# Top-k attention with two MoE layers on one core: order of the key rounding, the first unit's maxima, the norm's low part and the key splits

## The chip, the cores and the metric

The kernel runs on one core of one Trainium2 chip. The metric is device time in microseconds for one launch. The kernel before takes 1317.92 us, the median of three runs (1317.92 to 1319.5).

## The reference

For 4 batches of 8 heads with 576 positions of 64 elements: scores are `0.125 * q @ k.T`; in each row of scores only values not below the 32nd largest are kept; the row goes through a softmax and is multiplied with `v`. The heads are put side by side to `x` of 2304 tokens x 512. Then

```python
h = x @ w_in                      # 512 -> 2048
P = a0 + a1*h + a2*h**2 + a3*h**3
Q = 1 + |b0|*|h| + |b1|*h**2
x = (P / (Q + 1e-6)) @ w_out      # 2048 -> 512
h = x @ w_in2
out = (h * cos(h)) @ w_out2
```

All of it is float32. The second layer has weights of its own.

## The kernel before

Matrix products at full precision are made of three passes over values split into a rounded high part and a low part (`hi`, `lo`): high times high, high times low and low times high. Weights are split at the start by a converter (`conv`), which writes the low parts to DRAM, and keys by `split_k`: ScalarE rounds the raw keys into `hi`, GpSimd subtracts to get the low part, and four transfers on the queue of SyncE store both to the DRAM buffer `kdr`. The first 8 units use raw keys; later ones load the split keys back from `kdr`.

Work runs in 72 **units**. A unit is one tile of 128 queries with one pair of heads, in blocks of 8 units (four pairs by two tiles, 256 tokens). For each unit `qk` makes the scores in PSUM and ScalarE copies them to `sS`; `topk` on VectorE halves each row with a max and a min (`e<-sS`), finds the 32 largest with MAX8 and MATCH_REPLACE8, and multiplies the exponentials with the mask; `av` transposes the result on TensorE (the tiles `pp<i>a`, `pp<i>b`), copies it out (`pt`) and multiplies with `v`; `norm` divides by the sums and makes the high and low part of `x` (`xh`, `xl`). In between, each unit runs one step (256 tokens by 256 hidden columns) of each of the two layers: `in1` (products `h<-xh`, `h<-xl`), its polynomial on ScalarE, GpSimd and VectorE (`copy1`, `bias1`, `pol1`, `rec1`, `mid1`, `end1`, `low1`), `out1`, and `in2`, the cosine (`phase2`, `mid2`, `sin2`, `mul2`, `high2`, `low2`), `out2`.

Units 0 to 19 are ordered by a planner that puts ready instructions in order by a simulated time. From unit 20 to unit 71 every engine but SyncE keeps exactly the order in which `unit` writes its instructions: a wait of one holds back everything behind it on its engine. In that stretch GpSimd also waits for the last VectorE instruction written before it that shares its port, and the first VectorE instruction of a unit waits for GpSimd's last one of the unit before (`V.ahead = G.last`). That last one is `pol1`'s product `q<-q,r`.

Places that the change touches: in `unit`, the order `av`, `mid1` and `end1` (four VectorE operations and the rounding `gg<-u` on ScalarE), then `high2` (`gg<-rr`), `phase2`, the rounding of split keys, and only then the low parts kept in `low`, which are those of `norm`; `low` is filled in units 24, 32, ... and worked off in units 25, 33, 41, 49, 57 and 65, before `in1` of a new block needs `xl`. The rounding `xh<-xs` is written at the end of the unit before. `preps` says at the end of which unit raw keys are loaded for splitting; a load of an even unit is split in the odd unit behind it. For batch 2 these units are 24, 26, 28, 30 and for batch 3 40, 42, 44, 46 (so the splits are in 25, 27, 29, 31 and 41, 43, 45, 47). Units 29, 37, 45, ... also multiply the norm on GpSimd (`xs<-xs,bs`) and store a finished block from `ob`, of which there is one buffer.

The four places, in the lines of before: the rounding, `A.activation(hi, raw, AF.Copy)` in `split_k`; the table load, after the constants; `V.tensor_tensor(e[:, :, :HALF], l, r, op=ALU.max)` in `topk`; and in `unit`

```python
ev(i - UA - 1, mid1, end1)
...
for x in low:
    next(x, None)
low.clear()
```

Of the kernel before, what the change touches and what calls it, by code (L numbers as in the profile page):

```python
# [14 lines left out]
AF = mybir.ActivationFunctionType  # L15
ALU = mybir.AluOpType
# [12 lines left out]
HALF = S // 2  # L29
# [11 lines left out]
PL = 10  # L41
# [25 lines left out]
ORDER = mybir.DependencyInfo(mybir.DependencyClass.NoSync, mybir.DependencyReason.DATA)  # L67
# [52 lines left out]
def body(tc, out, qt, kt, vt, ident_d, w1_d, w1o_d, a_d, b_d, w2_d, w2o_d):  # L120
    nc = tc.nc
    V, A = InOrder(tc, nc.vector, WIN, C0), InOrder(tc, nc.scalar, WA, PA)
# [3 lines left out]
    with ExitStack() as ctx:  # L126
# [30 lines left out]
        sx = ps_s.tile([P, 2, 512], F32, name="sx")  # L157
# [5 lines left out]

        def split_k(x, b, pr):
            raw, hi = x[:, 0].bitcast(F32), x[:, 1]
            A.activation(hi, raw, AF.Copy)
            yield
            G.tensor_sub(raw, raw, hi.bitcast(F32))
            hi = hi.bitcast(F32)
            top, bot = slice(0, D), slice(D, P)  # L170
            d = kdr[b, pr]
            for o, i_ in ((d[top, 0], hi[top]), (d[bot, 0], raw[top]), (d[bot, 1], hi[bot]), (d[top, 1], raw[bot])):
                SP.dma_start(out=o, in_=i_)

        def store_k(*a):
            for _ in split_k(*a):
                pass
# [3 lines left out]
            SP.dma_start(out=x[:, 0].bitcast(F32), in_=kt[b, pr])  # L181
            return x

        qs_, vlast = {}, [None]

        def load_q(i):
            if i < nu:
                k, pr = units[i][0] // 2, units[i][1]
                raw = att.tile([P, 2, P], F32, tag="qr", bufs=QRB, name=f"qr{i}")
                A.dma_start(out=raw, in_=qt[k, pr, :, :, i % 2 * P:(i % 2 + 1) * P])  # L190
                qs_[i] = [raw, None]
# [9 lines left out]
        def low_q(i, E):  # L201
            if QH <= i < nu:
                raw, x = qs_[i]
                E.tensor_sub(x[:, 1], raw, x[:, 0].bitcast(F32))

        def load_k(i):
            n, pr = units[i]
            if i % 2 and not mixed[i]:
                ins[i] = [list(x) for x in ins[i - 1]]
                return  # L210
            ins[i] = []
            for b, _ in qts[n]:
                if n < 2:
                    k = load_k0(pr)
                else:
                    k = kv.tile([P, 2, S], F32R, tag="k", bufs=KB, name=f"k{i}_{b}")
                    A.dma_start(out=k.bitcast(F32), in_=kdr[b, pr])
                ins[i].append([k, None])
# [11 lines left out]
        load_q(0)  # L230
        load_k(0)
        load_q(1)
        ident = cst.tile([P, P], F32)
        SP.dma_start(out=ident, in_=ident_d)
        nident = cst.tile([P, P], F32R)
# [11 lines left out]
        G.memset(magic, MAGIC)  # L247
        qc = cst.tile([P, 1], F32)
        G.memset(qc, QC)
        tc.keep_in_program_order(A.preload_act_table_set("natural_log_exp_and_others"))  # L250
        na0, na1, na2, na3 = (nega[:, i:i + 1] for i in range(4))
        b0, b1 = babs[:, 0:1], babs[:, 1:2]

# [65 lines left out]
        order = [[], []]  # L319

        def halves(ap):
            return ap.rearrange("p (a c) -> p a c", a=2)

        def after(mm, bank):
            for x in order[bank]:
                tc.add_manual_dep(mm.ins, x, mybir.DependencyInfo(mybir.DependencyClass.NoSync, mybir.DependencyReason.DATA), reason="bank")

        def qk(i):
            n, pr = units[i]
            raw, x = qs_.pop(i)  # L330
            hi, lo = (x[:, 0], x[:, 1]) if x is not None else (None, None)
            kvs = ins[i]
            m = P // len(kvs)
            st[i] = sb = att.tile([P, 2, S], F32, tag="sS", bufs=SB, name=f"sS{i}")
            for j in range(2):
                rows = slice(j * D, (j + 1) * D)
                for c, (k, _) in reversed(list(enumerate(kvs))):
                    qs = slice(0, (c + 1) * m)
                    for hf in range(2):
                        o = sx[qs, hf, :HALF]  # L340
                        hs = slice(hf * HALF, (hf + 1) * HALF)
                        if n < 2:
                            mm = PE.matmul(o, raw[rows, j, qs], k[rows, 0, hs].bitcast(F32), start=True, stop=True)
                            after(mm, hf)
                        elif i < QH:
                            mm = PE.matmul(o, raw[:, j, qs], k[:, j, hs].bitcast(F32), start=True, stop=True)
                            after(mm, hf)
                        else:
                            mm = PE.matmul(o, hi[:, j, qs], k[:, j, hs], start=True, stop=False, skip_group_check=True)
                            after(mm, hf)  # L350
                            mm = PE.matmul(o, lo[:, j, qs], k[:, j, hs], start=False, stop=True, skip_group_check=True)
                        order[hf] = [mm.ins.name]
                A.activation(halves(sb[:, j]), sx[:, :, :HALF], AF.Copy)
                if j == 0:
                    yield
            if n == 1:
                store_k(kvs[0][0], 0, pr)

        def topk(i):
            n, pr = units[i]  # L360
            sc = st.pop(i)
            tiles = [sc[:, j] for j in range(2)]
            e = att.tile([P, 2, S], F32, tag="e", bufs=EB, name=f"e{i}")
            et[i] = e
            kb, t = n // 2, n % 2
            if i % 8 == 0:
                sums[kb] = sml.tile([P, 2, H], F32, tag="sum", bufs=2, name=f"sum{kb}")
            sm = sums[kb][:, t]
            hds = sml.tile([P, 2, 32], F32, tag="hd", bufs=2, name=f"hd_{i}")
            hd = [hds[:, j] for j in range(2)]  # L370
            nb = sml.tile([P, 2], F32, tag="nb", bufs=2, name=f"nb_{i}")
            big = [e[:, j, :HALF] for j in range(2)]
            both = [e[:, j] for j in range(2)]

            def top(j, x, r):
                V.max(out=hd[j][:, 8 * r:8 * r + 8], in_=x[j])

            def drop(j, x, r):
                V.match_replace(out=x[j], in_to_replace=hd[j][:, 8 * r:8 * r + 8], in_values=x[j], imm_value=NEG)

            l, r = sc[:, :, :HALF], sc[:, :, HALF:]
            grouped = U0 <= i < U1
            V.tensor_tensor(e[:, :, :HALF], l, r, op=ALU.max)
            if not grouped:
                top(0, big, 0)
                yield
            V.tensor_tensor(e[:, :, HALF:], l, r, op=ALU.min)
            if not grouped:
                top(1, big, 0)
            yield  # L390
            first = ((top, big, 0), (drop, big, 0), (top, big, 1))
            for step in (first[0 if grouped else 1:], ((drop, big, 1), (top, both, 2)), ((drop, both, 2),)):
                for f, *x in step:
                    for j in range(2):
                        f(j, *x)
                yield
            for j, s in enumerate(tiles):
                top(j, both, 3)
                if j == 0:
                    A.activation(nb, hds[:, :, 0], AF.Copy, scale=-SCALE)  # L400
                A.activation(e[:, j], s, AF.Exp, bias=nb[:, j:j + 1], scale=SCALE)
            yield
            for j, s in enumerate(tiles):
                row = sm[:, 2 * pr + j:2 * pr + j + 1]
                V.scalar_tensor_tensor(e[:, j], s, hd[j][:, 31:32], e[:, j], op0=ALU.is_ge, op1=ALU.mult, accum_out=row)
                yield
# [274 lines left out]
        def out2b():  # L681
            for part, steps in rest2:
                part(steps)
            rest2.clear()
# [68 lines left out]
        def ev(x, *fs):  # L753
            if 0 <= x < NB * NG:
                for f in fs:
                    run_event((f, *divmod(x, NG)))
# [4 lines left out]
        preps = {}  # L761
        for b in range(1, B):
            for pr in range(NP):
                preps.setdefault(16 * b - PL + pr if b == 1 else 16 * b - PL + 2 + 2 * pr, []).append((b, pr))

        nrm, low, held, split, x2, ob = [], [], [], [], [], []

# [103 lines left out]
        def unit(i, prev):  # L871
# [7 lines left out]
            a = av(i - 1)  # L879
            next(a)  # L880
            out2b()
            ev(i - UA - 1, mid1, end1)
            if not sine:
                ev(i - UB - 3, high2)
# [2 lines left out]
                    split.append(split_k(x, *a_))  # L887
                    next(split[-1])
                held.clear()
            for x in low:  # L890
                next(x, None)
            low.clear()
            low_q(i + 2, V)
            if i % 4 == 0:
                nrm.append(norm((i - 1) // 8, (i - 1) // 4 % 2))
# [70 lines left out]
        for u in range(UB + NB * NG + 3):  # L966
            grouped = U0 <= u < U1
            f = free(u, prev) if not grouped and u <= nu else iter(())
            for p in range(5):
                x = 5 * u + p  # L970
# [53 lines left out]
```

## Time and profile before

| what | value |
|---|---|
| median of three runs | 1317.92 us |
| the profiled execution's own time | 1315.85 us |
| its span in the trace | 1314.0 us |
| TensorE busy | 1225.8 us (93%) |
| VectorE busy | 1155.0 us (88%) |
| ScalarE busy | 1072.1 us (82%) |
| GpSimd busy | 586.0 us (45%) |
| mean granted TensorE clock | 0.969 |

The page divides the span into 40 slices and groups the instructions by what they read and write. Almost all lie on one line of the source (a helper that records every operation), so tiles tell them apart. The transposes `pp<i>a` mark on TensorE where the exponentials of unit i are taken up.

### The profile page before, as it was taken

To read this page: it belongs to the slowest core of one execution; us is meant where nothing else is said; L and a number is where in the kernel's file an instruction comes from. 1 tells how busy PE (TensorE), PEld (TensorE's weight loads), DVE (VectorE), ACT (ScalarE), POOL (GpSimd) and SP (SyncE) were. 2 spreads that over 40 slices of the span, in tenths; PEclk is the share of its full clock that TensorE was granted. 3 is DMA by queue.
4 is the path that set the end of the run, shared out by engine and by line. 5 is a ranking of instruction groups with operands and counts; after the bars stand their busy time and mean duration, and the time that the engine had idled before them with its cause. 6 is when DMAs were issued, how large, how long until landed. Compare 5 with 4: busy or idle time off the path is not lost.

```text
span 1314.0 us, 25152 instructions
## 1 busy us (share of the span) xinstructions
PE 1225.8 (93%) x8992; PEld 1079.5 (82%) x8992; DVE 1155.0 (88%) x2498; ACT 1072.1 (82%) x1839; POOL 586.0 (45%) x501
## 2 busy tenths in 40 slices
PE   6687788899999999999999999999999999999998
PEld 3344466678899989899989899999999999999996
DVE  6899999999899999999999899999999898756643
ACT  7887777777889888888888888988888888877753
POOL 2667556643454454545444454544454444430000
PEclk9766999999999999999999999999999999999999
DMA  8898778764367777666677776676666778867674
GB/s 292 294 345 254 246 257 276 251 240 157 130 210 231 254 253 235 205 212 230 224 240 238 240 228 200 223 230 216 218 246 251 280 275 296 289 227 249 228 269 151
DMA packets 120109, 314.99 MB, mean 240 GB/s; under 512 B 12592, under 2 KB 39344, under 8 KB 119984
## 3 DMA queue, kind: packets, MB, share of 16 engines
q1 hardware_dynamic: 86992, 261.99, 58.6%
q10 hardware_dynamic: 32992, 51.39, 12.1%
q8 instruction: 71, 1.16, 0.4%
q14 instruction: 54, 0.44, 0.1%
HBM read 278.20 MB, written 35.13 MB: 238 GB/s over the span
## 4 chain that ended last, share of the span: by engine, by line
PE 61%; DVE 12%; ACT 12%; DMA 7%; issue 4%; POOL 3%; ACTq 1%; SPq 0%; POOLq 0%; DVEq 0%
PE h L80 25%; PE o L80 11%; PE y L80 10%; PE sx L80 10%; DVE e L80 6%; DVE hd L80 3%; DMA raw<-w 2%; ACT r L80 2%; DVE u L80 2%; ACT raw L80 1%; ACT sS L80 1%; ACT e L80 1%; DMA raw<-w2o 1%; DMA kdr<-kraw 1%; PE diff L80 1%
## 5 line engine op out<-in xcount | busy, mean ns | idle before, releaser
L80 DVE MAX8 hd<-e 128x8 f32<-128x288 f32 (+1 forms) x576 | 320.5, 595 | 0.0
L80 POOL TENSOR_TENSOR gg<-rr,gg 128x512 fp32r<-128x512 f32 x56 | 72.5, 1295 | 387.1 <-DVE rr L80 184.4
L80 DVE MATCH_REPLACE8 e<-hd,e 128x288 f32<-128x288 f32 (+1 forms) x432 | 230.6, 540 | 0.0
L80 PE MATMUL o<-w2o,gg 128*128 128x512 f32 x864 | 223.6, 398 | 1.0 <-ACT ob L80 1.0
L80 PE MATMUL y<-gg,w1o 128*128 128x256 f32 x1152 | 215.2, 285 | 2.9 <-ACT gg L80 1.4
L80 PEld LDWEIGHTS y<-gg,w1o 128*128 128x128 f32 x1152 | 181.2, 191 | 6.6 <-POOL gg L80 2.6
L80 PEld LDWEIGHTS o<-w2o,gg 128*128 128x128 f32 x864 | 153.7, 189 | 28.0 <-ACT ob L80 1.2
L80 PE MATMUL h<-xh,w1hi 128*128 128x256 f32 x576 | 170.8, 297 | 3.9 <-ACT pt20a L80 0.6
L80 PE MATMUL h<-xl,w1hi 128*128 128x256 f32 x576 | 163.5, 284 | 3.5 <-DVE xl L80 3.5
L80 PE MATMUL y<-gg,w1ol 128*128 128x256 f32 x576 | 163.7, 284 | 0.0
L80 PE MATMUL h<-xh,lo 128*128 128x256 f32 x576 | 163.3, 283 | 0.0
L80 PE MATMUL h<-x2l,w2hi 128*128 128x256 f32 x576 | 161.5, 280 | 0.0
L80 PE MATMUL h<-x2h,w2hi 128*128 128x256 f32 x576 | 161.5, 281 | 0.0
L80 PE MATMUL h<-x2h,lo 128*128 128x256 f32 x576 | 161.2, 280 | 0.0
L80 DVE TENSOR_TENSOR e<-sS 128x576 f32<-128x576 f32 x144 | 115.9, 845 | 41.5 <-POOL q L80 32.9
L80 DVE SCALAR_TENSOR_TENSOR e<-sS,hd,e 128x576 f32<-128x576 f32 x144 | 126.4, 905 | 5.8 <-ACT e L80 5.8
L80 PEld LDWEIGHTS h<-xh,w1hi 128*128 128x128 f32 x576 | 109.6, 190 | 17.5 <-issue 7.1
L80 PEld LDWEIGHTS h<-xl,w1hi 128*128 128x128 f32 x576 | 109.8, 191 | 7.7 <-DVE xl L80 5.3
L80 PEld LDWEIGHTS y<-gg,w1ol 128*128 128x128 f32 x576 | 110.4, 192 | 0.4 <-issue 0.3
L80 PEld LDWEIGHTS h<-xh,lo 128*128 128x128 f32 x576 | 109.7, 190 | 0.3 <-issue 0.3
L80 PEld LDWEIGHTS h<-x2l,w2hi 128*128 128x128 f32 x576 | 108.4, 188 | 0.6 <-issue 0.2
L80 PEld LDWEIGHTS h<-x2h,w2hi 128*128 128x128 f32 x576 | 108.4, 188 | 0.4
(1025 smaller groups left out, 3240.5 us busy)
## 6 DMA issues: line engine op xcount, KB each, us to landing
w2o<-w2o SPq DMA_DIRECT2D x144, 512.0 KB, 4.3
lo<-w1lo SPq DMA_DIRECT2D x72, 512.0 KB, 3.8
w1ol<-w1ol SPq DMA_DIRECT2D x72, 512.0 KB, 4.5
lo<-w2lo SPq DMA_DIRECT2D x72, 512.0 KB, 4.4
k<-kdr ACTq DMA_DIRECT2D x44, 576.0 KB, 5.4
raw<-w SPq DMA_DIRECT2D x32, 512.0 KB, 6.1
v<-vt ACTq DMA_DIRECT2D x48, 320.0 KB, 3.8
qr<-qt ACTq DMA_DIRECT2D x72, 128.0 KB, 3.3
```

The lines of the kernel that those rows point to most:

```text
L80: r = f(*a, **k)
```

## The change

The rounding of the keys of batch 0 is ordered behind the last copy of scores made so far. ScalarE's table load is written ahead of the constants. In unit 0 the max and the min are written for each head by itself. The low part of the norm is written ahead of `mid1` and `end1`. The third and fourth pair of batches 2 and 3 are loaded for splitting in units 30 and 32, and 46 and 48, in place of 28 and 30, and 44 and 46; their splits are so in 31 and 33, and 47 and 49.

```diff
         def split_k(x, b, pr):
             raw, hi = x[:, 0].bitcast(F32), x[:, 1]
-            A.activation(hi, raw, AF.Copy)
+            r = A.activation(hi, raw, AF.Copy)
+            if b == 0:
+                tc.add_manual_dep(r.ins, copied[0], ORDER, reason="order")
             yield
...
         load_q(1)
+        tc.keep_in_program_order(A.preload_act_table_set("natural_log_exp_and_others"))
         ident = cst.tile([P, P], F32)
...
-        tc.keep_in_program_order(A.preload_act_table_set("natural_log_exp_and_others"))
         na0, na1, na2, na3 = (nega[:, i:i + 1] for i in range(4))
...
-                A.activation(halves(sb[:, j]), sx[:, :, :HALF], AF.Copy)
+                copied[0] = A.activation(halves(sb[:, j]), sx[:, :, :HALF], AF.Copy).ins.name
...
-            V.tensor_tensor(e[:, :, :HALF], l, r, op=ALU.max)
+            each = [slice(j, j + 1) for j in range(2)] if i == 0 else [slice(0, 2)]
+            for j in each:
+                V.tensor_tensor(e[:, j, :HALF], l[:, j], r[:, j], op=ALU.max)
...
-            V.tensor_tensor(e[:, :, HALF:], l, r, op=ALU.min)
+            for j in each:
+                V.tensor_tensor(e[:, j, HALF:], l[:, j], r[:, j], op=ALU.min)
...
-                preps.setdefault(16 * b - PL + pr if b == 1 else 16 * b - PL + 2 + 2 * pr, []).append((b, pr))
+                preps.setdefault(16 * b - PL + pr if b == 1 else 16 * b - PL + (2, 4, 8, 10)[pr], []).append((b, pr))
...
             out2b()
+            for x in low:
+                next(x, None)
+            low.clear()
             ev(i - UA - 1, mid1, end1)
...
-            for x in low:
-                next(x, None)
-            low.clear()
             low_q(i + 2, V)
```

## Rows read from the trace of the kernel before

**Rows 1.** Units 0-19, 20-71: length, busy PE, PEld, DVE, ACT, POOL, clock, DMA, GB/s.

```profile
0.00:330.75 330.75, 262.31 (x1369) 181.49 (x1370) 306.53 (x646) 257.42 (x485) 180.28 (x157) 0.88 0.78 260
330.75:1124.31 793.56, 780.34 (x6302) 727.70 (x6301) 743.89 (x1681) 690.21 (x1171) 381.50 (x326) 1.00 0.69 232
```

**Rows 2.** Timeline of the start: start, length, engine, operation, [idle before <- releaser].

```profile
7.12 1.28 ACT L80 ACT_TABLE_LOAD   x1
9.40 0.68 ACT L80 ACTIVATE kraw<-kraw 128x576 fp32r<-128x576 f32 x1 [1.00 <-DMA kraw<-kt]
9.99 0.63 ACT L80 ACTIVATE sS<-sx 128x576 f32<-128x576 f32 x1
...
19.30 0.63 ACT L80 ACTIVATE sS<-sx 128x576 f32<-128x576 f32 x1
...
10.65 1.43 DVE L80 TENSOR_TENSOR e<-sS 128x576 f32<-128x576 f32 x2 [5.18 <-ACT sS L80]
...
7.06 2.29 PE L80 MATMUL sx<-kraw,qr 64*128 64x288 f32 x4 [0.74 <-ACT sS L80]
...
6.32 2.27 SPq L274 DMA_DIRECT2D raw<-w  x4
10.11 1.09 SPq L173 DMA_DIRECT2D kdr<-kraw  x2
```

**Rows 3.** The same columns between the transposes of two units, five pairs.

```profile
473.13:505.21 32.08, 30.33 (x240) 27.78 (x238) 28.86 (x65) 26.94 (x47) 16.47 (x14) 1.00 0.72 245
718.00:751.36 33.36, 30.57 (x240) 27.82 (x239) 28.88 (x65) 26.95 (x47) 16.47 (x14) 1.00 0.68 235
596.74:626.50 29.76, 29.76 (x240) 27.89 (x239) 28.69 (x65) 26.37 (x46) 15.06 (x13) 1.00 0.70 236
...
535.52:566.69 31.17, 30.16 (x239) 27.84 (x238) 30.61 (x70) 27.37 (x48) 13.90 (x12) 1.00 0.61 207
656.52:687.69 31.17, 30.16 (x239) 27.83 (x238) 30.40 (x69) 27.95 (x49) 15.20 (x13) 1.00 0.72 236
```

**Rows 4.** Timeline of units 29 and 45: GpSimd, VectorE, ScalarE.

```profile
482.58 1.45 POOL L80 TENSOR_TENSOR kraw<-kraw 128x576 f32<-128x576 f32 x1
...
486.91 1.43 DVE L80 TENSOR_TENSOR e<-sS 128x576 f32<-128x576 f32 x2 [1.73 <-POOL q L80]
...
731.92 0.60 ACT L80 ACTIVATE ob<-o 128x512 f32<-128x512 f32 x1 [3.85 <-DMA out<-ob]
```

**Rows 5.** Timeline of unit 41: VectorE, ScalarE, GpSimd, TensorE.

```profile
656.15 0.75 DVE L80 SCALAR_TENSOR_TENSOR u<-u,nega,w 128x512 f32<-128x512 f32 x1
...
659.12 1.29 DVE L80 TENSOR_TENSOR xl<-xs,xh 128x512 fp32r<-128x512 f32 x2
...
669.44 1.43 DVE L80 TENSOR_TENSOR e<-sS 128x576 f32<-128x576 f32 x2 [0.49 <-POOL q L80]
...
671.52 0.81 DVE L80 SCALAR_TENSOR_TENSOR e<-sS,hd,e 128x576 f32<-128x576 f32 x1
...
656.99 1.14 ACT L80 ACTIVATE xh<-xs 128x512 fp32r<-128x512 f32 x2
...
659.23 0.63 ACT L80 ACTIVATE gg<-u 128x512 fp32r<-128x512 f32 x1
659.77 0.62 ACT L80 ACTIVATE gg<-rr 128x512 fp32r<-128x512 f32 x1
...
660.90 1.29 POOL L80 TENSOR_TENSOR gg<-rr,gg 128x512 fp32r<-128x512 f32 x1 [7.61 <-DVE q L80]
...
668.10 1.30 POOL L80 TENSOR_TENSOR q<-q,r 128x512 f32<-128x512 f32 x1
...
659.85 0.39 PE L80 MATMUL h<-xl,w1hi 128*128 128x256 f32 x1 [0.69 <-DVE xl L80]
...
672.72 0.60 PE L80 MATMUL pp41b<-ident,e 128*128 128x128 f32 x4
...
675.14 0.38 PE L80 MATMUL h<-xh,w1hi 128*128 128x256 f32 x1 [0.32 <-ACT pt41a L80]
```

More of the change, by code (lines that the diff above doesn't have):

```diff
@@ L182, in prep @@
             return x
-        qs_, vlast = {}, [None]
+        qs_, vlast, copied = {}, [None], [None]
         def load_q(i):
```

## The prediction

> **What bounds the kernel now.** I read the page first, then busy time by stage, then the timeline of the stages that the change touches. On the page TensorE leads by a little over VectorE and ScalarE, but that is a mean over two different stages. In units 0 to 19 VectorE is busy 306.5 of 330.75 us and TensorE 262.3; in units 20 to 71 TensorE is busy 780.3 of 793.6 us at the full clock [rows 1]. So the first stage ends when VectorE gets through, and only an earlier start or a wait taken from it helps. In the second, time is to be had only from the 13 us in which TensorE stands still, or from what follows such a stop.
>
> The order in the second stage is fixed, so units with the same position in a block repeat one another. I measured them on TensorE, from the first transpose of one unit to that two units on. The bounds of the windows in [rows 3] are these starts.
>
> **The splits in units 29 and 45 (preps).** Units 29 and 30 take 32.08 us with 1.75 idle on TensorE; units 45 and 46, 33.36 with 2.79. Units 37 and 38 have the same place in their block and no split: 29.76 and no idle at all [rows 3]. The cause can be seen in unit 29: GpSimd has the norm's product and the split's subtraction (1.45 us) in one unit, its last operation ends late, and VectorE's first of unit 30 waits 1.73 us for it [rows 4]. In unit 45 the second copy to `ob` also waits 3.85 us for the store of the first [rows 4], which stands behind split stores on SyncE's queue. Taking the split away gives back 32.08 - 29.76 = 2.32 and 33.36 - 29.76 = 3.60, together 5.9 us.
>
> What moves must be paid elsewhere. Units 31 and 47 had a split before and keep one. The new places are units 33 and 49, first but one in their blocks, as units 25 and 41 are, which have a split already. Units 33 and 34 without a split take 31.17 us, units 41 and 42 with one also 31.17 [rows 3]. So with the old order in the unit the new place costs nothing: the rounding and the subtraction lie in ScalarE's and GpSimd's slack, and the four stores and the load are as many as before, only on another part of SyncE's queue. Term: -5.9 us. Bounds: 0, if the stall goes along with the split, and -5.9.
>
> **The low part of the norm ahead of the polynomial.** It is meant for a wait that the trace shows: TensorE stands 0.69 us before the first product with `xl` [rows 5]. If that were all that changed, units 25, 33, 41, 49, 57 and 65 could gain up to 31.17 - 29.76 = 1.4 us each with what follows. But `xl` is `x` less its rounding, and the rounding is late. In unit 41 VectorE comes to this place at 656.15; ScalarE rounds from 656.99 to 658.13 in two steps [rows 5]. VectorE keeps its order, so in place of the polynomial's first operation it now stands until about 657.6 and does both low parts by 658.9 (0.6 each). The polynomial, 2.7 us (four operations of some 0.67), ends at 661.6 in place of 659.2. What waits for that:
>
> - ScalarE's `gg<-u` starts at 661.6 and not 659.23 [rows 5], 2.4 later, and everything behind it on ScalarE with it: `gg<-rr`, ending 1.16 after its neighbour's start, is ready at 662.8.
> - GpSimd's first operation of the unit needs that `gg`: 662.9 and not 660.90, 2.0 later.
> - GpSimd then runs without a gap from 660.90 to the end of `q` at 669.40 [rows 5], since in a split unit it has the subtraction too. So it ends 2.0 later, at 671.4.
> - VectorE's first operation of the next unit waits for just this end: it already stands 0.49 for it at 669.44 [rows 5], and now comes at 671.5.
> - TensorE takes the second head's product, ready at 671.52 + 0.81 = 672.33, at 672.72 [rows 5]. Of the 2.0 us it feels 2.0 - 0.4 = 1.6 us; 0.3 of these go into a wait of 0.32 that it has a little later for ScalarE [rows 5].
>
> So TensorE loses 1.35 us against before, the 0.69 already given back. There are four such units, for 33 and 49 now have a split: 4 x 1.35 = 5.4. Unit 57 has no split; there GpSimd has room, VectorE itself is 1.2 later (657.66 less 656.15, less a wait of 0.3 in the polynomial that disappears), and since VectorE's next unit does not stand those 0.49 us for GpSimd, its lead there is 0.4 + 0.5 = 0.9: 1.2 - 0.9 - 0.3 = 0. Unit 65 has two batches in a unit; I take 0 from unit 57. Term: +5.4 us. Bounds: -1.4 x 6 = -8.4 if nothing behind notices, and +2.04 x 4 + 1.2 x 2 = +10.6 if TensorE feels the whole lateness.
>
> **The start (rounding, table load, unit 0 by head).** In the trace ScalarE rounds the second pair's keys at 9.40, and the second copy of scores waits behind it until 9.99; VectorE's first max begins at 10.65 [rows 2]. Without the rounding the copy starts when its matmuls end, 7.06 + 2.29 = 9.35 [rows 2], 0.6 earlier. By head, one max and one min (0.35 each, half of what 1.43 shows for two) lie in the time in which VectorE stands. VectorE so reaches the end of unit 0 at least 0.6 + 0.7 = 1.3 us earlier. But it then needs the second copy of unit 1, at 19.30 [rows 2], behind ScalarE's conversion of weights that wait for their load. SyncE issues two pairs of stores of rounded keys early, one of them ahead of the first weights at 6.32; the second, 1.09 us, goes out only when the rounding at 9.40 is done [rows 2]. With the rounding later these issues are gone from there; at 1.09 for the first pair as well (an estimate from the second), the weights come 1.1 us earlier. I take 1.1, the smaller of 1.1 and 1.3, and carry it whole to unit 20, since VectorE idles only 24 us of the stage, 10.65 of them before its first max. Bounds: -2.8 (the second group of weights, held from 6.32 + 2.27 = 8.59 to 11.2, comes that much earlier), and +2.7 (four roundings of 0.68, which before filled gaps, now stand where ScalarE has work, and the planner's order of the stage turns against it).
>
> The table load costs nothing either way: it runs from 7.12 to 8.40, and the next instruction of ScalarE then waits 1.00 us for a transfer [rows 2]. Written first, it fills the time before the first constants. The Trainium skill (ScalarE: Activation LUTs, What ACT_TABLE_LOAD costs) gives a load 1.28 us and a drain of some 1.38 behind it. The trace agrees on the load and shows no drain of that length: the rounding starts 2.28 us after the load's start. By the page the copy could not have begun before 9.78, and the move would be worth 0.4 us more.
>
> **The sum.** -5.9 + 5.4 - 1.1 = -1.6 us. The profiled execution took 1315.85 us, of which the span is 1314.0 and 1.85 lie around it; it becomes 1314.25 with a span of 1312.4. The median of the runs is 2.07 us above this execution, so on their scale the forecast is 1316.3 us. What a measurement of this kernel can tell from no change is about 0.2%, 2.6 us; this is less.
>
> **The rivals.**
>
> *The low part is a gain.* The planner's stage ends earlier or ScalarE is ahead, the rounding is done when VectorE comes, and TensorE loses neither the 0.69 us nor the slow restart of 0.24 behind it (31.17 - 29.76 is 1.41, of which 0.3 is the wait for ScalarE): 0.93 x 6 = 5.6. Then 1317.9 - 1.1 - 5.9 - 5.6 = 1305.3. For it speaks that TensorE does wait for `xl`; against it that the rounding's row shows no wait ahead of it [rows 5], so ScalarE comes to it straight from other work. It decides at a rounding before 656.2. In the Trainium skill (Perfetto Trace Analysis, Optimization Strategies) the advice is to shorten what the idle matmul engine waits for, which is this; the trace agrees that it waits, but not that VectorE could come sooner. 0.22.
>
> *VectorE does not catch up.* Slower than before: VectorE finds no idle time in the units behind (26, 34, 42, 50), so the 2.0 us are not taken from its lead over TensorE but paid in full, and its own 1.2 in the two units without a split: +10.6 in place of +5.4. Then 1317.9 - 1.1 - 5.9 + 10.6 = 1321.5. It decides where the lead of 0.4 us at the second head's transposes is already eaten by the unit before. For it speaks that VectorE is busy 744 of 794 us in the stage [rows 1], against it that TensorE is busy 780. 0.20.
>
> *The forecast* keeps 0.58, with its own range 1313 to 1319.5, mostly for the start.
>
> **How the numbers follow.** The range must leave out no more than 0.2: from 1306, inside the first rival, to 1321, inside the second. Faster by over 0.2% (below 1315.3): the first rival, 0.22, and the forecast's lower part, 0.20, where the start gives over 2.3 us: 0.42. Slower (above 1320.5): most of the second rival, 0.16, and 0.04 of the forecast where the start turns against it: 0.20. Within: 0.38.
>
> **What would show it.** Units 29 and 30 at 29.8 us between transposes, and units 45 and 46 too; no wait of the second `ob` copy for a store. In units 33, 41 and 49 VectorE waiting 1.4 us for `xh` ahead of `xl`, TensorE's wait for `xl` gone, GpSimd's last product 2 us later in the unit and TensorE idle before `pp41b`, with 32.5 us for the two units in place of 31.17. Unit 0's second copy at 9.35 and unit 1's first max near 18.9. The forecast is wrong if ScalarE's rounding of `x` moves, if the planner orders units 0 to 19 anew, or if the split costs time at its new place.

## The result, and the profile after

The changed kernel takes 1325.62 us, the median of six runs (1323.06 to 1328.7). The kernel before, on the same chip, takes 1317.6 (six runs). The ratio is 1.0067 with a 95% interval of 1.0044 to 1.009, so the change makes the kernel slower by 0.44 to 0.9%. The forecast was 1316.3 and its range ended at 1321. The profiled execution took 1323.33 us, with a span of 1321.5; the span before was 1314.0.

First the two stages after, in the columns of [rows 1]:

```profile
0.00:340.06 340.06, 270.22 (x1393) 188.63 (x1394) 303.34 (x651) 256.37 (x487) 182.20 (x159) 0.86 0.74 255
340.06:1131.69 791.63, 777.66 (x6278) 725.03 (x6276) 745.76 (x1678) 687.45 (x1167) 377.21 (x324) 1.00 0.69 232
```

The planner's stage is longer by 9.3 us, although VectorE works less in it (303.3 and 306.5 us). Part of that is given back at once: the first transpose of unit 21, the handover to the fixed order, stands at 356.50 us and stood at 350.84, which is 5.66 later. From there to the same place of unit 71 the changed kernel takes 775.19 us (to 1131.69) and the one before 773.47 (to 1124.31), 1.72 more. The forecast had -1.1 for the first and -0.5 for the second.

The pairs of units between transposes, in the order of [rows 3] (29/30, 45/46, 37/38, 33/34, 41/42), and a sixth, 57/58:

```profile
480.22:509.98 29.76, 29.76 (x240) 27.92 (x239) 28.68 (x65) 26.37 (x46) 15.07 (x13) 1.00 0.71 245
725.55:755.31 29.76, 29.76 (x239) 27.92 (x238) 28.67 (x65) 26.37 (x46) 15.07 (x13) 1.00 0.70 244
602.82:632.59 29.77, 29.77 (x239) 27.92 (x238) 28.70 (x65) 26.37 (x46) 15.06 (x13) 1.00 0.70 235
540.28:572.82 32.54, 30.53 (x240) 27.83 (x239) 30.88 (x69) 27.78 (x49) 15.12 (x13) 1.00 0.66 217
662.60:695.14 32.54, 30.53 (x239) 27.84 (x238) 30.88 (x67) 27.77 (x49) 15.12 (x13) 1.00 0.68 224
...
907.93:940.48 32.55, 30.56 (x240) 27.84 (x239) 31.36 (x69) 27.20 (x48) 13.75 (x12) 1.00 0.60 199
```

Units 29 and 45 have lost their stop entirely. Every pair that begins with a low part has gained one: TensorE is busy 30.53 of 32.54 us, before 30.16 of 31.17. Units 25/26 and 49/50 read like 41/42, and so does 57/58, which has no split; 65/66 goes from 33.29 to 34.01.

Unit 41 after, timeline by engine, with the columns of [rows 5]:

```profile
663.72 1.29 DVE L80 TENSOR_TENSOR xl<-xs,xh 128x512 fp32r<-128x512 f32 x2 [1.42 <-ACT xh L80]
...
677.49 1.43 DVE L80 TENSOR_TENSOR e<-sS 128x576 f32<-128x576 f32 x2 [0.48 <-POOL q L80]
...
679.57 0.82 DVE L80 SCALAR_TENSOR_TENSOR e<-sS,hd,e 128x576 f32<-128x576 f32 x1
...
667.70 0.64 ACT L80 ACTIVATE gg<-u 128x512 fp32r<-128x512 f32 x1 [2.36 <-DVE u L80]
...
670.71 0.25 ACT L80 ACTIVATE xs<-sx 128x128 f32<-128x128 f32 x1
...
671.11 0.77 PE L80 MATMUL sx<-k,q 128*128 128x288 f32 x4 [1.68 <-ACT xs L80]
...
679.80 0.63 PE L80 MATMUL pp41a<-ident,e 128*128 128x128 f32 x4 [0.31 <-DVE e L80]
680.45 0.65 PE L80 MATMUL pp41b<-ident,e 128*128 128x128 f32 x4
```

The copy `xs` and the scores behind it in the kernel before, which the prediction did not look at:

```profile
662.72 0.28 ACT L80 ACTIVATE xs<-sx 128x128 f32<-128x128 f32 x1 [0.40 <-PE sx L80]
...
664.14 0.70 PE L80 MATMUL sx<-k,q 128*128 128x288 f32 x4
```

Read down the first fence: VectorE stands 1.42 us for `xh`, so the polynomial ends late and ScalarE stands 2.36 us for it ahead of `gg<-u`. Behind `gg<-u` on ScalarE is the copy `xs<-sx`. The next scores (`sx<-k,q`) overwrite what it reads, and TensorE stands 1.68 us for the copy. Before, ScalarE itself waited for TensorE at that copy, and the scores followed without an idle moment. Counted from the unit's first transpose (656.52 before, 662.60 after), the copy starts 6.20 us behind it before and 8.11 after, 1.91 later. The wait for `xl` (0.69 before [rows 5]) is gone, so TensorE comes 0.69 earlier. The spare time was 664.14 - 663.00 = 1.14, less the 0.15 that still pass after the copy. 1.91 + 0.69 - 0.99 = 1.6, close to the new wait of 1.68.

This wait is where TensorE's loss is seen, but it does not set the length of the pair. Behind it TensorE still stands 0.31 us for VectorE at `pp41a`. VectorE's second product, which `pp41b` transposes, ends 17.79 us behind the first transpose (15.81 before [rows 5]), and `pp41b` starts 0.06 behind that end, at 17.85 (16.20 before). VectorE comes late because it stands for GpSimd's `q`, 0.48 us, and GpSimd runs without a gap from 668.99 to that point; neither waits for these scores in between. So by the rows, without the wait at the scores TensorE would have stood 1.99 us at `pp41a`, and the pair would be as long.

The start after:

```profile
2.11 1.28 ACT L80 ACT_TABLE_LOAD   x1 [2.11 <-issue]
...
4.40 2.30 SPq L276 DMA_DIRECT2D raw<-w  x4
...
7.07 0.83 DVE L80 TENSOR_TENSOR e<-sS 128x288 f32<-128x288 f32 x2 [1.43 <-ACT sS L80]
...
9.41 0.65 ACT L80 ACTIVATE sS<-sx 128x576 f32<-128x576 f32 x1 [2.28 <-PE sx L80]
...
18.19 2.65 DVE L80 TENSOR_TENSOR e<-sS 128x576 f32<-128x576 f32 x2
```

Here the edits do what they say. The second copy comes at 9.41 instead of 9.99, the weights are issued at 4.40 instead of 6.32, and VectorE starts at 7.07 instead of 10.65 [rows 2]. Unit 1's first max comes at 18.19, 1.77 us earlier than the 19.96 of before. At unit 7 the kernel is ahead: its transposes come at 115.75 and came at 120.98. It is still 1.3 us ahead at unit 18, but 8.9 behind at unit 19 and 5.66 behind at unit 21: from unit 18 to unit 21 it takes 56.0 us, the kernel before 49.0.

### The profile page after: what moved, and what is told of

It is laid out like the page before. It is cut to its first block, busy times and chain, and to the rows that moved or that the text cites. A ratio compares the mean times of both kernels' runs of the same rounds, so it can differ in the third digit from the quotient of the medians.

```text
span 1321.5 us, 25151 instructions
## 1 busy us (share of the span) xinstructions
PE 1231.0 (93%) x8992; PEld 1084.0 (82%) x8992; DVE 1153.8 (87%) x2500; ACT 1068.4 (81%) x1838; POOL 583.6 (44%) x501
## 4 chain that ended last, share of the span: by engine, by line
PE 60%; DVE 14%; ACT 11%; POOL 5%; DMA 5%; issue 4%; ACTq 0%; SPq 0%; POOLq 0%; DVEq 0%
PE h L80 24%; PE o L80 12%; PE y L80 10%; PE sx L80 10%; DVE e L80 6%; DVE u L80 3%; DVE hd L80 3%; DMA raw<-w 2%; ACT r L80 2%; PE diff L80 2%; ACT raw L80 1%; ACT sS L80 1%; ACT e L80 1%; POOL q L80 1%; DVE raw L80 1%
## 5 line engine op out<-in xcount | busy, mean ns | idle before, releaser
L80 PE MATMUL y<-gg,w1o 128*128 128x256 f32 x1152 | 218.3, 288 | 4.1 <-POOL gg L80 2.6
L80 DVE TENSOR_TENSOR e<-sS 128x576 f32<-128x576 f32 (+1 forms) x146 | 113.3, 817 | 43.5 <-POOL q L80 27.2
L80 DVE SCALAR_TENSOR_TENSOR e<-sS,hd,e 128x576 f32<-128x576 f32 x144 | 123.1, 885 | 9.2 <-ACT e L80 9.1
L80 ACT ACTIVATE e<-sS,nb 128x576 f32<-128x576 f32 x144 | 105.8, 772 | 11.7 <-DVE hd L80 10.1
```

The lines of the kernel that those rows point to most:

```text
L80: r = f(*a, **k)
```

## The experiments

"Unit 21" below is the time in the span at which TensorE starts that unit's transposes. In the traces of six kernels that have the order of before up to there (before, the moved preparation alone, the low part alone, the low part later, `xh` earlier, the table load alone) it lies between 349.60 and 354.19 us, so a few us of it are scatter. (Unit 21 transposes the exponentials of unit 20, the tiles `pp20a`; some of the expectations call the same mark the first transpose of unit 20.) Each ratio is to runs of the kernel before on the same chip.

### Which part costs: the four parts apart

**The moved preparation alone**, on the kernel before:

```diff
-                preps.setdefault(16 * b - PL + pr if b == 1 else 16 * b - PL + 2 + 2 * pr, []).append((b, pr))
+                preps.setdefault(16 * b - PL + pr if b == 1 else 16 * b - PL + (2, 4, 8, 10)[pr], []).append((b, pr))
```

> The kernel before with the moved key splits alone. Theory A (the parts add up): units 29 and 30, and 45 and 46, take 29.8 us between transposes in place of 32.08 and 33.36, units 33 and 34 stay at 31.2, and the span falls by 5.9 us to 1308.1, a ratio of 0.9955. Theory B (the split's cost goes along): units 33/34 and 49/50 grow by what 29/30 and 45/46 lose, and the span stays within 1.5 us of 1314.0.

Measured: 1310.76 us, ratio 0.9961 [0.9945, 0.9976], span 1308.8. Units 29/30, 45/46 and 33/34:

```profile
473.73:503.51 29.78, 29.78 (x240) 27.91 (x239) 28.69 (x65) 26.37 (x46) 15.09 (x13) 1.00 0.75 244
716.29:746.07 29.78, 29.78 (x239) 27.91 (x238) 28.68 (x65) 26.38 (x46) 15.09 (x13) 1.00 0.72 243
533.81:564.99 31.18, 30.17 (x240) 27.83 (x239) 30.62 (x69) 27.96 (x49) 15.18 (x13) 1.00 0.74 226
```

The stalls go, and the split costs nothing in its new place.

**The low part first alone**, on the kernel before:

```diff
             out2b()
+            for x in low:
+                next(x, None)
+            low.clear()
             ev(i - UA - 1, mid1, end1)
...
                 held.clear()
-            for x in low:
-                next(x, None)
-            low.clear()
```

> The kernel before with the low part of the norm ahead of the polynomial, alone. Theory A (VectorE stands for the late rounding of x and everything behind the polynomial is late, with or without a split): each of the pairs 25/26, 33/34, 41/42, 49/50 and 57/58 goes from 31.17 to 32.5 us, 65/66 grows by 0.7, and the span grows by 7.4 us to 1321.4, ratio 1.0056. Theory B, as predicted: only the units with a split (25, 41) lose 1.35, the others nothing, span 1316.7, ratio 1.002. Theory C (the wait of 0.69 us is all): the span falls by 5.6 us.

Measured: 1324.72 us, ratio 1.0069 [1.0048, 1.009], span 1320.9. Units 25/26, 33/34, 41/42, 49/50 and 57/58 all take 32.5 us. Unit 33 has no split here and 41 has one, so GpSimd's subtraction is not what sets the price.

**The three edits of the start together** (the rounding's ordering edge, the table load, the maxima by head):

```diff
+            if b == 0:
+                tc.add_manual_dep(r.ins, copied[0], ORDER, reason="order")
...
+        tc.keep_in_program_order(A.preload_act_table_set("natural_log_exp_and_others"))
         ident = cst.tile([P, P], F32)
...
+            each = [slice(j, j + 1) for j in range(2)] if i == 0 else [slice(0, 2)]
```

> The kernel before with the three edits of the start alone (rounding behind the scores' copies, table load first, unit 0 by head). Theory A (the planner orders units 0 to 19 anew and loses time by it): unit 1's first max still comes near 18.2 us in place of 19.96, but the first transpose of unit 20 comes 5.7 us later than 350.84, and the span is 1319.7, ratio 1.0043. Theory B (the start gains, and what was lost in units 1 to 20 came from the other edits): the transpose comes at 349.1 to 349.7, the span is 1312.3 to 1312.9.

Measured: 1325.6 us, ratio 1.0076 [1.0055, 1.0097], span 1324.5; unit 21 at 359.08. That is 8.2 us later than before, more than the 5.7 of theory A. The start costs as much as the whole change.

**The whole change without the low part's new place** (the loop over `low` back behind `held.clear()`):

```diff
-            for x in low:
-                next(x, None)
-            low.clear()
             ev(i - UA - 1, mid1, end1)
```

> The changed kernel with the norm's low part back behind the polynomial. Theory A (parts add up): 7.4 us less than the changed kernel, span 1314.1, ratio to the kernel before 1.000. Theory B (the new place of the splits is dear with either order): pairs 33/34 and 49/50 at over 32 us, span over 1315.5.

Measured: 1318.62 us, ratio 1.0019 [1.0002, 1.0035], span 1318.0; unit 21 at 360.34, units 33/34 and 49/50 at 31.17. The start's loss remains, and the moved preparation gives most of it back. The span is 3.9 us above theory A because this execution comes to unit 21 3.84 later than that of the whole change, with the same order up to there.

### Why the low part costs

**The low part two operations later**: the kernel with the moved preparation, the low part written between the second and the third operation of the polynomial, and in those units `gg<-rr` ahead of the polynomial's last two (`end1` is cut in two for it).

```diff
-            ev(i - UA - 1, mid1, end1)
+            ev(i - UA - 1, mid1)
+            if low:
+                ev(i - UB - 3, high2)
+            ev(i - UA - 1, end1a)
+            early = bool(low)
+            for x in low:
+                next(x, None)
+            low.clear()
+            ev(i - UA - 1, end1b)
```

> The moved splits, and in the units that make it the norm's low part between the second and the third of the polynomial's four operations on VectorE, with the rounding of the cosine's product ahead of the polynomial's on ScalarE. Theory A (VectorE stood for the late rounding of x, and GpSimd started late for want of the second layer's rounding): no wait for xh, none of TensorE for xl, GpSimd starts within 0.4 us of its old place, pairs 33/34 and 41/42 at 30.6 to 31.1 us, span 1308.8 less 1 to 3. Theory B (two more VectorE operations ahead of the polynomial's end are dear wherever they stand): the pairs stay over 32 us, span over 1312.

Measured: 1309.2 us, ratio 0.9932 [0.9913, 0.9951], span 1308.1. The five pairs take 30.56 or 30.57 us, 0.6 less than before. Unit 41:

```profile
654.58 1.29 DVE L80 TENSOR_TENSOR xl<-xs,xh 128x512 fp32r<-128x512 f32 x2
...
657.29 0.63 ACT L80 ACTIVATE gg<-u 128x512 fp32r<-128x512 f32 x1 [0.65 <-DVE u L80]
...
660.17 0.77 PE L80 MATMUL sx<-k,q 128*128 128x288 f32 x4
```

VectorE no longer stands for `xh`, ScalarE stands 0.65 us instead of 2.36, and the scores wait for nothing. The wait for `xl` is gone as well, since `xl` still comes two operations earlier than before. The span is just above the range given (1305.8 to 1307.8), in a trace whose units 69/70 take 32.73 us against 30.87 with the moved preparation alone; the cause of that was not followed.

**`xh` rounded earlier**: the low part first, as in the change, with the moved preparation; in the units that begin a block, `xh<-xs` is issued on ScalarE ahead of the reciprocal's evaluation (`r<-q,qc` and `r<-r`).

```diff
-            ev(i - UA, rec1)
             if i % 8 == 0:
                 for x in nrm:
                     next(x)
                 low.extend(nrm)
                 nrm.clear()
+            ev(i - UA, rec1)
```

> Before with the split keys' moved preparation and the low part ahead of the polynomial, and in the units that carry a polynomial xh's rounding issued on ScalarE ahead of that unit's reciprocal evaluation. Theory A, the loss of 1.36 us in each such pair comes from the low part's place on VectorE, with TensorE's scores waiting for ScalarE's copy xs: the pairs stay at 32.4 to 32.6, span 1313 to 1317. Rival B, VectorE stands because xh's rounding comes late from ScalarE: the pairs fall to 30.8 to 31.3, span 1307 to 1311.

Measured: 1312.36 us, ratio 0.9969 [0.9956, 0.9981], span 1313.0. The pairs take 31.27 to 31.37, against 32.5. Unit 41:

```profile
657.87 1.29 DVE L80 TENSOR_TENSOR xl<-xs,xh 128x512 fp32r<-128x512 f32 x2 [0.16 <-ACT xh L80]
...
661.85 0.63 ACT L80 ACTIVATE gg<-u 128x512 fp32r<-128x512 f32 x1 [1.08 <-DVE u L80]
...
665.25 0.77 PE L80 MATMUL sx<-k,q 128*128 128x288 f32 x4 [0.39 <-ACT xs L80]
```

Theory A held that the place on VectorE costs whatever ScalarE does. By the pairs it falls: they stand at the edge of what rival B gave. The span doesn't decide, since this execution comes to unit 21 at 354.19, 3.35 later than the one of before; the pairs are taken behind that. The three kernels make a row: VectorE's wait is 1.42, 0.16 or 0 us, ScalarE's behind it 2.36, 1.08 or 0.65, TensorE's at the scores 1.68, 0.39 or 0. VectorE's second product ends 17.79, 16.52 or 15.82 us behind the first transpose, and the pair takes 32.54, 31.3 or 30.56. From the first kernel to the second only the rounding's place differs in these units, so the late rounding is the cause of the loss; the third kernel moves `gg<-rr` as well. The copy `xs` is not what carries it. That shows in units 57/58 of the kernel with the early rounding, where the scores wait for nothing and TensorE stands for VectorE at `pp57a` all the same:

```profile
907.60 0.76 PE L80 MATMUL sx<-k,q 128*128 128x288 f32 x4
...
916.30 0.63 PE L80 MATMUL pp57a<-ident,e 128*128 128x128 f32 x4 [0.31 <-DVE e L80]
```

This pair takes 31.29 us, no less than the others. What is late for TensorE is VectorE's product.

### Why the start costs

**The rounding's ordering edge alone.**

```diff
-            A.activation(hi, raw, AF.Copy)
+            r = A.activation(hi, raw, AF.Copy)
+            if b == 0:
+                tc.add_manual_dep(r.ins, copied[0], ORDER, reason="order")
```

> The kernel before with the rounding of batch 0's keys behind the scores' copies, alone. Theory A (unit 0 by head is what makes the planner order the stage anew and dear): unit 0's max comes near 10.05 in place of 10.65, the first transpose of unit 20 stays within 2 us of 350.8, span 1312 to 1315. Theory B (the four roundings and their stores, now late, cost the time): that transpose comes 5 us or more later, span 1319 or more.

**The table load alone.**

```diff
         load_q(1)
+        tc.keep_in_program_order(A.preload_act_table_set("natural_log_exp_and_others"))
         ident = cst.tile([P, P], F32)
...
-        tc.keep_in_program_order(A.preload_act_table_set("natural_log_exp_and_others"))
```

> The kernel before with the table load ahead of the constants, alone; the order of all other instructions is that of before. Both theories: one load of 1.28 us less on ScalarE, no change, transpose of unit 20 within 1.5 us of 350.8, span 1313 to 1315. It also shows how far two executions with the same order lie apart at unit 20.

**Unit 0's max and min by head alone.**

```diff
-            V.tensor_tensor(e[:, :, :HALF], l, r, op=ALU.max)
+            each = [slice(j, j + 1) for j in range(2)] if i == 0 else [slice(0, 2)]
+            for j in each:
+                V.tensor_tensor(e[:, j, :HALF], l[:, j], r[:, j], op=ALU.max)
```

> The kernel before with unit 0's max and min by head, alone. Theory A: the first max comes near 7.1 us, unit 1's first max 1 to 2 us earlier than 19.96, and yet the first transpose of unit 20 comes 5 us or more later than 350.8, span 1319 or more. Theory B: it comes no later than before, span 1314 or less.

| edit alone | median us | ratio | unit 7 | unit 21 |
|---|---|---|---|---|
| the kernel before | | | 120.98 | 350.84 |
| rounding | 1323.97 | 1.0047 [1.0032, 1.0063] | 118.30 | 359.38 |
| table load | 1317.9 | 1.000 [0.9988, 1.0011] | 121.73 | 352.91 |
| by head | 1316.15 | 0.9989 [0.9973, 1.0004] | 117.50 | 353.00 |

The loss belongs to the rounding's edge, and my suspicion of the edit by head fell. The marks at unit 21 of the table load and of the maxima by head lie 2.1 and 2.2 us behind that of before, outside what was expected for them (within 1.5; 5 or more, or none), but inside the range above, and their ratios are 1.000 and 0.9989. But the kernel with the edge is 2.7 us ahead at unit 7, by when batch 0's roundings are made (the last starts at 118.81 us), and loses 11 us only behind it. The edge does two things: it makes four roundings late, and it makes the planner put the other instructions of units 0 to 19 in another order. The next two kernels take these apart.

**The roundings late, everything else in the order of before.** Each instruction of units 0 to 19 gets an ordering edge to the next on its engine, in the order of before; the roundings and the stores of their results are left free, and the change's edge is in.

```diff
+        for text in PINS.values():
+            at = was = None
+            for step in text.split():
+                at = int(step) + (at or 0)
+                name = f"I-{at}"
+                if name in MADE:
+                    if was is not None:
+                        tc.add_manual_dep(MADE[name], was, ORDER, reason="pin")
+                    was = name
```

> Before with the roundings of batch 0's keys late, as in the change, but with every other instruction of units 0 to 19 on TensorE, VectorE, GpSimd, ScalarE and SyncE held in the order that the kernel before has (an ordering edge from each to the next on its engine); alone, the rounding edit lets the planner put 312 places of VectorE's order otherwise. Theory A, the planner's other order costs the time and not the late roundings: TensorE reaches unit 21 at 348 to 353 us of the span (before 350.84, the rounding edit alone 359.38), the span is 1312 to 1317. Rival B, the late roundings themselves (their keys' stores, or what they push back on ScalarE) cost it: unit 21 at 356 or later, span 1319 or more.

**The roundings early, everything else in the order that the edge had brought.** The same lines with the other list, and without the change's edge.

> The reverse: before with batch 0's keys rounded early, as before has them, and every other instruction of units 0 to 19 held in the order that the rounding edit alone had given. Theory A, the order costs the time: unit 21 at 356 to 360, span 1319 to 1323. Rival B, the late roundings cost it: unit 21 at 348 to 353, span 1312 to 1317.

Measured: with the roundings late and the order of before, 1317.8 us, ratio 1.0007 [0.9996, 1.0019], unit 21 at 354.58, span 1317.5. With the roundings early and the other order, 1324.7 us, ratio 1.0061 [1.0042, 1.008], unit 21 at 359.19, span 1322.2. The order costs what the edge costs, with or without the late roundings. The first kernel's unit 21 and span lie just outside what theory A gave, 1.6 and 0.5 us above, so a small cost of the late roundings isn't excluded; by its interval it is at most 0.19%.

Windows up to unit 7 and from there to unit 21, in the columns of [rows 1]; first before:

```profile
0.00:120.98 120.98, 84.73 (x261) 45.71 (x261) 103.24 (x221) 100.50 (x188) 67.13 (x59) 0.77 0.87 299
120.98:350.84 229.86, 195.65 (x1252) 152.20 (x1253) 218.22 (x459) 173.77 (x325) 121.93 (x106) 0.95 0.69 228
```

With the roundings late in the order of before, the second of these stretches takes 230.64 us, and VectorE is busy 218.17 of it.

The roundings early in the other order:

```profile
0.00:119.32 119.32, 82.08 (x257) 43.72 (x257) 104.69 (x218) 95.70 (x180) 61.09 (x54) 0.80 0.85 292
119.32:359.19 239.87, 201.26 (x1257) 156.04 (x1256) 216.13 (x462) 177.90 (x335) 127.61 (x111) 0.92 0.69 225
```

The work is the same: VectorE is busy 321.5 us to unit 21 before and 320.8 in the other order, but stands 29.4 and 38.4 us. What it stands for is shown by the waits between 119 and 357 us (total, times, longest). Of before:

```profile
DVE raw L80 <- ACT raw L80: 5.5, 6, 1.5
...
DVE e L80 <- ACT e L80: 0.8, 1, 0.8
```

In the other order:

```profile
DVE raw L99 <- ACT raw L99: 7.9, 6, 2.5
DVE e L99 <- ACT e L99: 7.2, 6, 1.9
DVE rr L99 <- ACT n L99: 5.3, 1, 5.3
```

VectorE waits for ScalarE's exponentials 7.2 us instead of 0.8. The single wait of 5.3 us for the cosine's `n` is new as well, but it comes late, in unit 20, where VectorE of before stands 1.9 and 3.2 us for other things; 7.3 of the 8.3 us are lost by unit 18. ScalarE in turn stands for weights that it converts. Its waits between 119 and 340 us, before:

```profile
ACT raw L80 <- DMA raw<-w: 6.7, 5, 1.8
ACT raw L80 <- DMA raw<-w2o: 5.9, 7, 2.2
```

In the other order:

```profile
ACT raw L99 <- DMA raw<-w: 11.0, 9, 2.9
ACT raw L99 <- DMA raw<-w2o: 7.2, 5, 2.6
```

That is 18.2 us against 12.6, and with the edge alone it is 17.2. With the late roundings in the order of before it is 12.7. So in the other order ScalarE comes to conversions before their weights have landed, and exponentials stand behind them. Whether the conversions came sooner or their loads later was not told apart. That this wait carries the whole loss is read from the rows and was not tried by itself.

### The change with both steps mended

**Without the rounding's edge, and with the low part two operations later**; the maxima by head, the table load and the moved preparation stay as in the change.

```diff
-            if b == 0:
-                tc.add_manual_dep(r.ins, copied[0], ORDER, reason="order")
...
+            ev(i - UA - 1, end1a)
+            early = bool(low)
             for x in low:
                 next(x, None)
             low.clear()
-            ev(i - UA - 1, mid1, end1)
+            ev(i - UA - 1, end1b)
```

> The change with two of its steps altered: without the ordering edge on batch 0's rounding, and with the low part two operations later (between the second and the third operation of the polynomial, as in the kernel with the moved preparation and the low part there). It keeps the first unit's maxima by head, the earlier table load and the moved preparation. Theory, what the change lost lies in these two steps alone: TensorE reaches unit 21 at 349 to 354 us of the span, the pairs 25/26, 33/34, 41/42, 49/50 and 57/58 stand at 30.5 to 30.7, the span is 1306 to 1312, ratio 0.992 to 0.996. Rival, any edit of the first units that moves the planner costs as the rounding's edge did: unit 21 at 356 or later, span 1314 or more, ratio 0.997 or more.

Measured: 1306.18 us (six runs, 1303.7 to 1306.99), ratio 0.9921 [0.9902, 0.994]. It beats both kernels. Unit 21 stands at 347.94 and the span is 1302.1, both better than the range given; the ratio and the pairs met theirs. Unit 41/42:

```profile
650.08:680.64 30.56, 30.50 (x239) 27.84 (x238) 29.77 (x67) 27.88 (x49) 15.16 (x13) 1.00 0.73 239
```

This kernel's early order differs from before's, too, and does not cost: on TensorE, VectorE and GpSimd it is that of the kernel with the maxima by head alone, whose unit 21 stands at 353.00. So it isn't every new order that costs.

## Why the prediction was wrong

The terms of the sum, and what the trace of the changed kernel shows for each:

| term | predicted us | measured us |
|---|---|---|
| splits out of units 29 and 45 | -5.9 | -2.32 - 3.60 = -5.92 |
| low part, units 25, 33, 41, 49 | 4 x 1.35 = +5.4 | 1.35 + 3 x 1.37 = +5.46 |
| low part, units 57 and 65 | 0 | 1.36 + 0.72 = +2.08 |
| the start, at unit 21 | -1.1 | +5.66 |
| sum | -1.6 | +7.3 |

The span grew by 7.5. The start's 5.66 is that of one execution: the two other kernels with the change's order up to unit 21 (the start's three edits, and the whole change without the low part) come there at 359.08 and 360.34, 8.2 and 9.5 later than before.

**The start is the step that failed.** "I take 1.1, the smaller of 1.1 and 1.3, and carry it whole to unit 20" was right for the first units (1.77 at unit 1) and wrong in being carried. The stage is put in order anew when one edge is added. The edge alone costs 6.3 us by the medians, and its order without the late roundings 8.1. The prediction named this twice, in the term's upper bound ("the planner's order of the stage turns against it") and in its last sentence, but priced it by the four roundings, 2.7 us. The price of another order isn't that of what is moved: the late roundings themselves cost next to nothing, while VectorE stands 9 us longer. This step alone puts the time beyond the range: 1316.3 + 5.66 + 1.1 = 1323.1. In the whole change, too, it is the edge that costs: the three kernels with its early order reach unit 21 at 356.50, 359.08 and 360.34, and the two that have the maxima by head without the edge (alone, and in the mended kernel) at 353.00 and 347.94. What is not settled is which wait carries the loss there. That early order is a third one, ScalarE's waits for weights are 9.4 us in it and not more than before, and order and late roundings were taken apart only for the edge alone. The rows say where to look: from unit 18 to unit 21 the three kernels take 6.5 to 7.0 us longer than the one before, and VectorE's longest wait there is for scores of TensorE, 6.42 us in the changed kernel and 5.97 and 6.02 in the two others:

```profile
335.29 1.43 DVE L80 TENSOR_TENSOR e<-sS 128x576 f32<-128x576 f32 x2 [6.42 <-PE sx L80]
```

The kernel before has no such wait; the two kernels without the edge have one of 5.97 and 5.79, but as early as unit 7. That it carries the loss was not tried.

**The low part was right in the units with a split and failed in those without.** In unit 41 the chain that the prediction wrote down took place to its end: VectorE's wait for `xh` (predicted 1.4, measured 1.42), `gg<-u` counted from the first transpose (2.71 before, 5.10 after, 2.4 later as predicted), GpSimd's `gg` (4.38 and 6.39, predicted 2.0 later), VectorE's first operation behind GpSimd's `q` (12.92 and 14.89, predicted 2.0 later) and `pp41b` (16.20 and 17.85, predicted 1.6 later). Only the stop is seen elsewhere. TensorE was to stand ahead of `pp41b`, and stands 1.68 ahead of the scores and 0.31 ahead of `pp41a`. The copy `xs`, for which it stands first, is a wait that the prediction never considered, since it followed `gg<-u` to GpSimd and not to what ScalarE does behind it; here it takes nothing that the transposes would not have taken.

For unit 57, "1.2 - 0.9 - 0.3 = 0" is the second step that failed. Before:

```profile
909.10 1.02 DVE L80 SCALAR_TENSOR_TENSOR rr<-n,rr 128x512 f32<-128x512 f32 x1
...
917.20 0.81 DVE L80 SCALAR_TENSOR_TENSOR e<-sS,hd,e 128x576 f32<-128x576 f32 x1
...
918.88 0.60 PE L80 MATMUL pp57b<-ident,e 128*128 128x128 f32 x4
...
921.29 0.38 PE L80 MATMUL h<-xh,w1hi 128*128 128x256 f32 x1 [0.32 <-ACT pt57a L80]
```

After:

```profile
915.60 1.79 DVE L80 SCALAR_TENSOR_TENSOR rr<-n,rr 128x512 f32<-128x512 f32 x1
...
924.34 0.82 DVE L80 SCALAR_TENSOR_TENSOR e<-sS,hd,e 128x576 f32<-128x576 f32 x1
...
925.22 0.66 PE L80 MATMUL pp57b<-ident,e 128*128 128x128 f32 x4
...
927.93 0.39 PE L80 MATMUL h<-xh,w1hi 128*128 128x256 f32 x1 [0.56 <-ACT pt57a L80]
```

Counted from the first transpose (902.66 and 907.93), VectorE's second product ends at 15.35 before and 17.23 after, 1.88 later and not 1.2: `rr<-n,rr` takes 0.77 longer there, which the last section explains. The lead was right; 0.81 of it is used. The wait of 0.32 behind does not disappear but grows to 0.56. 1.88 - 0.81 + 0.24 = 1.31, of 1.36 measured. TensorE stands 1.11 us of this for the copy `xs` and then 0.30 for VectorE at `pp57a`. Unit 65, which the prediction took from unit 57, was not followed.

The rival "VectorE does not catch up" came nearest with 1321.5, and unit 57 is a part of it: VectorE's own lateness is paid there beyond its lead. The rival "the low part is a gain" did not come about at this place, but did so in part two operations later, where each pair gains 0.6 us.

**The splits were right** in size, place and cause: 29.76 us in units 29 and 45 without a stop, and no cost in 33 and 49, as the kernel with this part alone shows.

**The table load** costs nothing either way, as predicted. The prediction saw only the load at 7.12; there is one at 2.76, too, and with the move a single one is left, at 2.11. As an estimate from the figures of the Trainium skill (ScalarE: Activation LUTs, What ACT_TABLE_LOAD costs) the move would be worth 0.4 us; the interval of that kernel, 0.9988 to 1.0011, can't tell this from nothing.

## What to carry to other kernels

Before an instruction is moved ahead on an engine that keeps its order, look at when its input is ready in the trace; then follow what comes late on every engine to everything queued behind it, a buffer's release included, up to the wait that ends last. An earlier stop on the same engine only takes its share of that one, and mending it alone gives nothing back. Where a planner orders a stage, an edit there has two prices, that of the edit and that of the new order; pinning the old order with the edit in, and the new order without it, separates them. And where the parts of a change have different signs, take them one by one: a gain of 0.4% stood here behind two losses of 0.5% and 0.7%, and the parts, sorted, gave a kernel that is 0.8% faster than the one before.

## What the hardware showed unexpectedly

One VectorE operation, `rr<-n,rr` with two inputs in SBUF, takes three lengths. In unit 42 of before, with GpSimd idle beside it, 0.68 us (at 676.45); in unit 41 of before, beginning in the middle of a GpSimd product, 1.03 (at 662.96); in unit 41 after, beginning within 0.04 us of the start of one, 1.78:

```profile
670.26 1.78 DVE L80 SCALAR_TENSOR_TENSOR rr<-n,rr 128x512 f32<-128x512 f32 x1
...
670.22 1.27 POOL L80 TENSOR_TENSOR gg<-u,gg 128x512 fp32r<-128x512 f32 x1
671.45 1.76 POOL L80 TENSOR_TENSOR rr<-rr,hs 128x512 f32<-128x512 f32 x1
```

Its length is the rest of GpSimd's product plus half a us, as if it began when that ended: 671.49 + 0.55 is the 672.04 at which it ends. The Trainium skill (GPSIMD Engine Reference, Specifications) says that GpSimd shares its SBUF interfaces with VectorE, with contention where a VectorE instruction has two inputs in SBUF; these rows agree. So the new order cost VectorE another 0.75 us in this unit, and as much in units 25, 33 and 49. There it was hidden, since VectorE still stood 0.47 to 0.49 us for GpSimd's `q` behind it. In unit 57, where VectorE does not wait for GpSimd, it was not, and it is more than half of what that pair lost.
